# Attention, expert layers and a gated layer on one core: another order of the constant buffers in SBUF

## The chip, the cores and the metric

The kernel runs on one NeuronCore of a Trainium2 chip. The metric is the device time of one execution in microseconds (us). A core has five engines with a queue each: TensorE (PE, matrix products, its weight loads shown as PEld), VectorE (DVE), ScalarE (ACT), GpSimd (POOL) and SyncE (SP, which here only issues DMAs). SBUF is the on-chip memory; a tile takes the same range of bytes in each of 128 partitions, and an address below is an offset in KB inside a partition, as the built program has it.

In a product, PE first loads the *held* operand (up to 128 columns, the `lhsT` of a call), then streams the *moved* operand (`rhs`, 384 or 512 columns) past it. The profile writes `bank<-moved,held`.

## The reference, cut to what matters

```python
def _moe_ref(x, w_gate, w1, w2):            # 1536 tokens, D 512, E 8 experts, F 1024
    P = ...                                 # gates: softmax of x @ w_gate, 8 Sinkhorn rounds
    for e in range(E):
        h = np.maximum(x @ w1[e], 0.0)      # first products, relu
        out += P[:, e:e+1] * (h @ w2[e])    # second products
    return out

def _moe2_ref(x, w_gate, w_val, w_out):     # 512 -> 1536 -> 512
    gate = 1.0 / (1.0 + np.exp(-(x @ w_gate)))
    val = x @ w_val                         # first products, two of them
    return gate * val @ w_out               # second products

def reference(**kwargs):
    x = _attn_ref(...)                      # banded attention, 2 x 8 heads, 768 positions
    return _moe2_ref(_moe_ref(x, ...), ...)
```

## The kernel before

Every large product is done in three passes on pairs of float32r parts (high and low): `product` (lines 360 to 370) emits, for each slice of the contraction, high x high (L368), high x low (L369 moves the low part) and low x high (L370 holds the low part). So each matmul has a weight load of its own, and lines 368 to 370 carry nearly all of PE's work.

The work falls into *visits*, one for each quarter of an expert's hidden width or each sixth of the gated layer's. In a visit **first products** hold slices of a weight tile (`wh[slot][0]`, `wl[slot][0]`) and move tokens (`xh`, `xl`); their results become the hidden pair `hh`, `hl`. **Second products** hold slices of `hh`, `hl` and move the output weights (`wh[slot][1]`, `wl[slot][1]`, 512 columns) into an accumulator `acc`. Second products of one unit run behind the first products of the next.

- Expert 0 runs in plain visits (`run_visit`): first products of 12 matmuls with 384 columns, second products of 6 with 512 columns. The gate's logits (L1166, L1170, held tile `wg2`) lie among them.
- Experts 1 to 7 run in 28 fast visits (`run_fast`, `pair`), each of two halves. A half has 7 products of 6 matmuls with 384 columns, which move `xh`/`xl` or the transformed tokens `th`/`tl` and hold slices (`form`) of `wh00`, `wl00`, `wh10`, `wl10`, and 6 second products of 6 matmuls with 512 columns: 78 matmuls. The order is written out in `pair`.
- The last (gated) layer has 6 blocks of three chunks of 512 tokens. In a chunk, 48 first products with 512 columns are followed by the 24 second products of the chunk before. Even blocks hold `wh*0`/`wl*0`; odd blocks hold four tiles of a pool of their own (`wgh`, `wgl`, `wvh`, `wvl`). The layer's hidden pairs (`hid.extend`, L1302) are also tiles of that pool, `hh0`, `hl0`, `hh1`, `hl1`. The pool (`glu`) opens on the space of the fast visits' pool.

Tiles get addresses in the order in which a pool makes them. The order of instructions is the order of the calls; nothing is rescheduled.

Of the kernel before, what the change touches and what calls it, by code (L numbers as in the profile page):

```python
# [9 lines left out]
F32 = mybir.dt.float32  # L10
F32R = mybir.dt.float32r
# [6 lines left out]
P = 128  # L18
# [7 lines left out]
HID = 3  # L26
# [40 lines left out]
def tile_global_local_attention__then__sinkhorn_moe__then__glu(  # L67
# [27 lines left out]
    E, _, F = w1.shape  # L95
# [3 lines left out]
    KD = DM // P  # L99
# [3 lines left out]
    C = TC * P  # L103
    CM = 4 * P
    CB = S // C
    FQ = 2 * P
# [7 lines left out]
    const = ctx.enter_context(tc.tile_pool(name="const", bufs=1))  # L114
# [5 lines left out]
    ones = const.tile([P, P], F32, name="ones")  # L120
    xh = const.tile([P, KD, N], F32R, name="xh")
    xl = const.tile([P, KD, N], F32R, name="xl")
    accs = [const.tile([P, TB, DM], F32, name="acc0")]
    hh3 = const.tile([P, HID, 2, C], F32R, name="hh3")
    hl3 = const.tile([P, HID, 2, C], F32R, name="hl3")
    hid = [(hh3[:, i], hl3[:, i]) for i in range(HID)]
    wh = [[const.tile([P, 4 * FQ], F32R, name=f"wh{i}{j}") for j in range(2)] for i in range(2)]
    wl = [[const.tile([P, 4 * FQ], F32R, name=f"wl{i}{j}") for j in range(2)] for i in range(2)]
    raw = [const.tile([P, 8 * FQ], F32, name=f"raw{i}") for i in range(2)]

    dram = ctx.enter_context(tc.tile_pool(name="dram", bufs=1, space=bass.MemoryType.DRAM))
    glw = [dram.tile([P, 4 * FQ], F32, name=f"glw{i}") for i in range(3 * NFF)]
    wgr = const.tile([P, KD, E], F32, name="wgr")
    wg2 = const.tile([P, KD, 2 * E], F32R, name="wg2")

    def acc(t):
        return accs[t // TB][:, t % TB, :]
# [490 lines left out]
    with tc.tile_pool(name="attn", bufs=1) as ap:  # L628
# [79 lines left out]
        for h in range(H):  # L708
            j = h % 2
# [270 lines left out]
        with cmp.Else():  # L980
            with tc.tile_pool(name="whole", bufs=1) as gp:
# [15 lines left out]
                for s in range(B * NP):  # L997
                    b, p = divmod(s, NP)
# [16 lines left out]
                    for i in range(NB):  # L1015
# [29 lines left out]
                        for j in range(2):  # L1045
                            h = 2 * (s % NP) + j
# [245 lines left out]
    for step in glu_split[3:6]:  # L1292
# [4 lines left out]
    glu = ctx.enter_context(tc.tile_pool(name="glu", bufs=1))  # L1297
# [1 line left out]
        tuple(glu.tile([P, 4 * FQ], F32R, name=f"w{j}{x}") for x in "hl") for j in "gv"  # L1299
    )  # L1300
    state["glu_hid"] = 0
    hid.extend(  # L1302
        tuple(glu.tile([P, 2, CM], F32R, name=f"h{x}{i}") for x in "hl") for i in range(2)
    )
    state["sg"] = Ring(glu.tile([P, CM], F32, name=f"sg{i}") for i in range(2))
    state["z"] = Ring(glu.tile([P, CM], F32, name=f"z{i}") for i in range(2))
    state["o"] = Ring(glu.tile([P, DM], F32, name=f"o{i}") for i in range(3))
# [57 lines left out]
```

## Time and profile before

| | us |
|---|---|
| median of 3 runs | 1451.95 |
| lowest, highest | 1450.70, 1451.98 |
| the profiled execution's own time | 1453.22 |
| its span, first to last instruction | 1450.7 |

The page of the profile gives each engine's busy time and 40 slices of the span; its chain follows the work that ended last backwards. In the timeline each row is an instruction: start, duration, engine, line, operation, operands and shape. A matmul's duration is modelled and reaches past the start of the next; the distance between two starts is what PE takes for one. Grouped views add instructions of one line and shape up: how many, their busy time, the mean of one.

### The profile page before, as it was taken

To read this page: it belongs to the slowest core of one execution; us is meant where nothing else is said; L and a number is where in the kernel's file an instruction comes from. 1 tells how busy PE (TensorE), PEld (TensorE's weight loads), DVE (VectorE), ACT (ScalarE), POOL (GpSimd) and SP (SyncE) were. 2 spreads that over 40 slices of the span, in tenths; PEclk is the share of its full clock that TensorE was granted. 3 is DMA by queue.
4 is the path that set the end of the run, shared out by engine and by line. 5 is a ranking of instruction groups with operands and counts; after the bars stand their busy time and mean duration, and the time that the engine had idled before them with its cause. 6 is when DMAs were issued, how large, how long until landed. Compare 5 with 4: busy or idle time off the path is not lost.

```text
span 1450.7 us, 19810 instructions
## 1 busy us (share of the span) xinstructions
PE 1432.3 (99%) x7287; PEld 1231.5 (85%) x7287; DVE 863.0 (59%) x1655; ACT 505.3 (35%) x1152; POOL 568.1 (39%) x618
## 2 busy tenths in 40 slices
PE   8999999999999999999999999999999999999998
PEld 4666788999999999999899899899999888888887
DVE  6576477676657666767676666666665533333333
ACT  5777322433333333333333333333333322122111
POOL 3555354554344454354454444445432221112110
PEclk9999999999999999999999999999999999999999
DMA  7661011122121222221212212212210110010002
GB/s 178 160 144 45 17 45 58 45 102 73 52 73 52 73 79 75 73 73 51 73 52 102 73 53 72 73 52 102 73 37 29 44 45 15 30 44 30 0 1 87
DMA packets 99192, 92.60 MB, mean 64 GB/s; under 512 B 55312, under 2 KB 73744, under 8 KB 99088
## 3 DMA queue, kind: packets, MB, share of 16 engines
q1 hardware_dynamic: 98800, 91.26, 20.3%
q8 instruction: 59, 0.97, 0.3%
q14 instruction: 45, 0.37, 0.1%
q10 hardware_dynamic: 288, 0.00, 0.0%
HBM read 78.66 MB, written 12.58 MB: 63 GB/s over the span
## 4 chain that ended last, share of the span: by engine, by line
PE 95%; DVE 2%; ACT 1%; POOL 1%; issue 1%; DMA 0%; DVEq 0%; ACTq 0%; SPq 0%; POOLq 0%
PE bank L368 30%; PE bank L370 30%; PE bank L369 30%; PE bank L867 1%; PE bank L919 1%; PE bank L905 1%; PE bank L841 1%; ACT e L881 1%; DVE e L875 0%; POOL wl L202 0%; PE bank L1313 0%; POOL e L893 0%; DMA lens<-in_n_local_dram 0%; DMA qr<-in_q_dram 0%; DVE kT L845 0%
## 5 line engine op out<-in xcount | busy, mean ns | idle before, releaser
L451 DVE SCALAR_TENSOR_TENSOR acc<-bank,gate,acc 128x512 f32<-128x512 f32 x336 | 251.6, 749 | 234.4 <-PE bank L370 232.1
L370 PE MATMUL bank<-wh,hl 128*128 128x512 f32 x912 | 359.6, 394 | 0.0
L368 PE MATMUL bank<-wh,hh 128*128 128x512 f32 x912 | 359.1, 394 | 0.0
L202 POOL TENSOR_TENSOR wl<-raw,wh 128x512 fp32r<-128x512 f32 (+1 forms) x196 | 209.7, 1086 | 380.3 <-ACT wh L201 380.1
L369 PE MATMUL bank<-wl,hh 128*128 128x512 f32 x912 | 358.0, 392 | 0.0
L368 PE MATMUL bank<-xh,wh 128*128 128x384 f32 (+1 forms) x720 | 252.9, 351 | 1.3 <-ACT aT L906 1.1
L370 PE MATMUL bank<-xh,wl 128*128 128x384 f32 (+1 forms) x720 | 251.2, 349 | 0.0
L369 PE MATMUL bank<-xl,wh 128*128 128x384 f32 (+1 forms) x720 | 250.1, 347 | 0.0
L370 PEld LDWEIGHTS bank<-wh,hl 128*128 128x128 f32 x912 | 171.2, 188 | 38.3
L546 ACT ACTIVATE hh<-kept 128x384 fp32r<-128x384 f32 x168 | 88.2, 525 | 312.1 <-DVE kept L556 312.1
L368 PEld LDWEIGHTS bank<-wh,hh 128*128 128x128 f32 x912 | 171.6, 188 | 27.8 <-issue 1.3
L369 PEld LDWEIGHTS bank<-wl,hh 128*128 128x128 f32 x912 | 171.5, 188 | 26.9
L368 PEld LDWEIGHTS bank<-xh,wh 128*128 128x128 f32 x720 | 135.4, 188 | 15.5 <-issue 1.3
L369 PEld LDWEIGHTS bank<-xl,wh 128*128 128x128 f32 x720 | 135.3, 188 | 13.5 <-DVE xl L1318 0.5
L370 PEld LDWEIGHTS bank<-xh,wl 128*128 128x128 f32 x720 | 135.1, 188 | 5.7
L202 POOL TENSOR_TENSOR wl<-work,wh 128x256 fp32r<-128x256 f32 x112 | 93.8, 839 | 99.6 <-ACT wh L201 96.9
L560 ACT ACTIVATE kept<-bank 128x384 f32<-128x384 f32 x168 | 82.3, 491 | 120.1 <-PE bank L370 120.0
L548 DVE SCALAR_TENSOR_TENSOR hl<-kept,hh 128x384 fp32r<-128x384 f32 x168 | 112.3, 669 | 1.3 <-ACT hh L546 1.3
L370 PE MATMUL bank<-th,wl 128*128 128x384 f32 x336 | 113.1, 337 | 0.0
L368 PE MATMUL bank<-th,wh 128*128 128x384 f32 x336 | 112.5, 335 | 0.0
L369 PE MATMUL bank<-tl,wh 128*128 128x384 f32 x336 | 112.4, 335 | 0.0
L426 DVE TENSOR_TENSOR z<-bank,sg 128x512 f32<-128x512 f32 x36 | 24.9, 691 | 139.3 <-PE bank L370 139.3
(143 smaller groups left out, 1862.2 us busy)
## 6 DMA issues: line engine op xcount, KB each, us to landing
raw<-in_moe_w_dram SPq DMA_DIRECT2D x72, 512.0 KB, 4.3
glw<-work SPq DMA_DIRECT2D x36, 256.0 KB, 2.3
raw<-glw SPq DMA_DIRECT2D x18, 512.0 KB, 3.3
work<-in_moe_w_gate_dram SPq DMA_DIRECT2D x12, 512.0 KB, 4.0
work<-in_moe_w_val_dram SPq DMA_DIRECT2D x12, 512.0 KB, 3.8
work<-in_moe_w_out_dram SPq DMA_DIRECT2D x12, 512.0 KB, 3.8
qr<-in_q_dram SPq DMA_DIRECT2D x32, 96.0 KB, 2.9
kr<-in_k_dram SPq DMA_DIRECT2D x32, 96.0 KB, 2.7
```

Source lines behind the costliest of these rows:

```text
L202: nc.gpsimd.tensor_tensor(out=lo, in0=r, in1=h.bitcast(F32), op=ALU.subtract)
L368: nc.tensor.matmul(lhsT=ah, rhs=bh, start=first, stop=False, **mm)
L369: nc.tensor.matmul(lhsT=ah, rhs=bl, start=False, stop=False, **mm)
L370: nc.tensor.matmul(lhsT=al, rhs=bh, start=False, stop=end, **mm)
L426: nc.vector.tensor_tensor(out=z, in0=ps, in1=sg, op=ALU.mult)
L451: nc.vector.scalar_tensor_tensor(out=a, in0=ps, scalar=gate[:, t, e : e + 1], in1=a, op0=ALU.mult, op1=ALU.add,)
L546: nc.scalar.activation(out=hh[:, f, :C], in_=src, func=AF.Relu)
L548: lambda: nc.vector.scalar_tensor_tensor(out=hl[:, f, :C], in0=src, scalar=0.0, in1=hh[:, f, :C].bitcast(F32), op0=ALU.max, op1=ALU.subtract,)
L560: nc.scalar.activation(out=snap[:, i], in_=ps, func=AF.Copy)
L841: nc.tensor.transpose(ps[:, j * P : (j + 1) * P], raw_[u % QKB][:, j, :], ident)
L867: nc.tensor.matmul(out=ps[j][:, lo:KW], lhsT=qT[rows, own], rhs=kT[rows, keys], start=True, stop=True,)
L881: nc.scalar.activation(out=e[:, j, lo:KW], in_=e[:, j, lo:KW], func=AF.Exp, scale=-1.0, bias=mn[:, j : j + 1], accum_out=rs[:, j : j + 1],)
```

## The change

The constant tiles are made in another order, `hh3`/`hl3` become flat tiles that `hidden_parts` cuts up, and the last layer's two hidden pairs are cut from them too instead of being tiles of the last layer's pool. The addresses in KB of each partition, from the built programs:

| tiles | role | before | after |
|---|---|---|---|
| xh, xl | moved in first products | 17.12 to 65.12 | the same |
| wh01, wl01, wh11, wl11 | moved in second products | 99.12 to 103.12, 115.12 to 119.12, 107.12 to 111.12, 123.12 to 127.12 | 65.12 to 81.12 |
| acc0 | accumulator | 65.12 to 77.12 | 81.12 to 93.12 |
| wgr, wg2 | gate weights, wg2 held | 143.12 to 143.50 | 93.12 to 93.50 |
| hh3, hl3 | held in second products | 77.12 to 95.12 | 93.50 to 111.50 |
| wh00, wl00, wh10, wl10 | held in first products | 95.12 to 99.12, 111.12 to 115.12, 103.12 to 107.12, 119.12 to 123.12 | 111.50 to 127.50 |
| raw0, raw1 | weights as loaded | 127.12 to 143.12 | 127.50 to 143.50 |
| last layer's wgh, wgl, wvh, wvl | held in first products, odd blocks | 156.44 to 172.44 | the same |
| last layer's hh, hl | held in second products | 172.44 to 188.44 | in hh3, hl3 |
| last layer's sg, z, o | scratch | 188.44 to 202.44 | 172.44 to 186.44 |
| th, tl | moved in fast visits | 177.44 to 213.44 | the same |
| acc1 | accumulator | 143.50 to 155.50 | the same |

A multiple of 512 bytes is a multiple of half a KB: a start at .12 is 128 bytes past one, at .44 448 bytes, at .50 none; wg2 starts 256 bytes past one in both.

```diff
+    wh, wl = ([[None, None] for _ in range(2)] for _ in range(2))
+    def weight_tiles(j):
+        for i in range(2):
+            wh[i][j] = const.tile([P, 4 * FQ], F32R, name=f"wh{i}{j}")
+            wl[i][j] = const.tile([P, 4 * FQ], F32R, name=f"wl{i}{j}")
+    weight_tiles(1)
     accs = [const.tile([P, TB, DM], F32, name="acc0")]
-    hh3 = const.tile([P, HID, 2, C], F32R, name="hh3")
-    hl3 = const.tile([P, HID, 2, C], F32R, name="hl3")
-    hid = [(hh3[:, i], hl3[:, i]) for i in range(HID)]
-    wh = [[const.tile([P, 4 * FQ], F32R, name=f"wh{i}{j}") for j in range(2)] for i in range(2)]
-    wl = [[const.tile([P, 4 * FQ], F32R, name=f"wl{i}{j}") for j in range(2)] for i in range(2)]
+    wgr = const.tile([P, KD, E], F32, name="wgr")
+    wg2 = const.tile([P, KD, 2 * E], F32R, name="wg2")
+    hh3 = const.tile([P, HID * 2 * C], F32R, name="hh3")
+    hl3 = const.tile([P, HID * 2 * C], F32R, name="hl3")
+    def hidden_parts(count, m):
+        h, lo = (
+            x[:, 0 : count * 2 * m].rearrange("p (i f m) -> p i f m", i=count, f=2)
+            for x in (hh3, hl3)
+        )
+        return [(h[:, i], lo[:, i]) for i in range(count)]
+    hid = hidden_parts(HID, C)
+    weight_tiles(0)
     raw = [const.tile([P, 8 * FQ], F32, name=f"raw{i}") for i in range(2)]
...
-    wgr = const.tile([P, KD, E], F32, name="wgr")
-    wg2 = const.tile([P, KD, 2 * E], F32R, name="wg2")
...
-    hid.extend(
-        tuple(glu.tile([P, 2, CM], F32R, name=f"h{x}{i}") for x in "hl") for i in range(2)
-    )
+    hid.extend(hidden_parts(2, CM))
```

On every engine the instructions and their order stay as they were. One set of waits moves on PE: that for everything that used the space on which the last layer's pool opens. It stands with the first instruction of PE that reads a tile of that pool. Before, this is the first second product behind the transposes of `acc` (the numbers in the names are the program's own: wh_81 is wh11, hh_12296 the last layer's hh0):

```order
L1313 MATMUL bank_70<-ident,acc_4929 128x128 x3
L368 MATMUL bank_66<-wh_81,hh_12296 128x512 [waits DMAHW4_49,DMAHW3_49,DMAHW5_49,DMAHW2_49,DMAHW6_49,DMAHW1_49,DMAHW7_49,DMAHW0_49,PE_49]
L369 MATMUL bank_66<-wl_85,hh_12296 128x512
L370 MATMUL bank_66<-wh_81,hl_12297 128x512
L368 MATMUL bank_66<-wh_81,hh_12296 128x512
```

In the changed kernel the same place reads a part of hh3 (hh_82, hl_83; wh_77 is wh11), which is no tile of that pool, and has no wait:

```order
L1329 MATMUL bank_70<-ident,acc_4929 128x128 x3
L386 MATMUL bank_66<-wh_77,hh_82 128x512
L387 MATMUL bank_66<-wl_78,hh_82 128x512
L388 MATMUL bank_66<-wh_77,hl_83 128x512
L386 MATMUL bank_66<-wh_77,hh_82 128x512
```

The waits now stand on PE before the first product of the first odd block:

```order
L388 MATMUL bank_67<-wh_77,hl_83 128x512
L386 MATMUL bank_63<-xh,wgh 128x512 [waits DMAHW4_49,DMAHW3_49,DMAHW5_49,DMAHW2_49,DMAHW6_49,DMAHW1_49,DMAHW7_49,DMAHW0_49,PE_49]
L387 MATMUL bank_63<-xl,wgh 128x512
L388 MATMUL bank_63<-xh,wgl 128x512 [waits Pool_49]
L386 MATMUL bank_63<-xh,wgh 128x512
```

Only these waits have moved, from the one place to the other.

## Rows read from the trace of the kernel before

**Rows 1.** Head of the page: busy us, share, instructions; granted clock in 40 slices.

```profile
PE 1432.3 (99%) x7287; PEld 1231.5 (85%) x7287; DVE 863.0 (59%) x1655; ACT 505.3 (35%) x1152; POOL 568.1 (39%) x618
...
PEclk9999999999999999999999999999999999999999
```

**Rows 2.** The page's chain that ended last, shares of the span by engine.

```profile
PE 95%; DVE 2%; ACT 1%; POOL 1%; issue 1%; DMA 0%; DVEq 0%; ACTq 0%; SPq 0%; POOLq 0%
```

**Rows 3.** Busy us by window, last layer: PE, PEld, DVE, ACT, POOL, clock, DMA.

```profile
1240.00:1290.00 50.00, 50.00 (x220) 40.98 (x219) 16.81 (x25) 10.51 (x18) 7.92 (x7) 1.00 0.10 32
```

**Rows 4.** Timeline of PE in the last layer: start us, duration us, instruction.

```profile
1257.55 0.39 PE L368 MATMUL bank<-xh,wh 128*128 128x512 f32 x1
...
1258.94 0.39 PE L368 MATMUL bank<-xh,wh 128*128 128x512 f32 x1
...
1263.02 0.39 PE L368 MATMUL bank<-xh,wh 128*128 128x512 f32 x1
...
1268.46 0.40 PE L368 MATMUL bank<-wh,hh 128*128 128x512 f32 x1
...
1284.97 0.40 PE L368 MATMUL bank<-wh,hh 128*128 128x512 f32 x1
...
1290.57 0.40 PE L368 MATMUL bank<-xh,wgh 128*128 128x512 f32 x1
...
1301.77 0.40 PE L368 MATMUL bank<-wh,hh 128*128 128x512 f32 x1
```

**Rows 5.** Groups of PE in the last layer (1160 to 1451 us): count, busy us, mean ns.

```profile
L368 PE MATMUL bank<-wh,hh 128*128 128x512 f32 x144 | 57.1, 396 | 0.0
...
L368 PE MATMUL bank<-xh,wh 128*128 128x512 f32 x123 | 48.1, 391 | 0.0
...
L368 PE MATMUL bank<-xh,wgh 128*128 128x512 f32 x72 | 28.5, 396 | 0.0
```

**Rows 6.** Timeline of PE from one logit group to the next (x4: four matmuls).

```profile
154.66 1.08 PE L1166 MATMUL bank<-xh,wg 128*16 128x512 f32 x4
...
156.51 0.40 PE L368 MATMUL bank<-wh,hh 128*128 128x512 f32 x1
...
157.89 1.10 PE L1166 MATMUL bank<-xh,wg 128*16 128x512 f32 x4
```

**Rows 7.** Timeline of PE in expert 0, first products of 384 columns.

```profile
208.73 0.33 PE L368 MATMUL bank<-xh,wh 128*128 128x384 f32 x1
...
209.80 0.33 PE L368 MATMUL bank<-xh,wh 128*128 128x384 f32 x1
...
210.97 0.42 PE L368 MATMUL bank<-xh,wh 128*128 128x384 f32 x1
211.23 0.34 PE L369 MATMUL bank<-xl,wh 128*128 128x384 f32 x1
...
212.48 0.33 PE L370 MATMUL bank<-xh,wl 128*128 128x384 f32 x1
```

**Rows 8.** Timeline of PE in a fast visit, the first and last from half to half.

```profile
756.05 0.33 PE L368 MATMUL bank<-xh,wh 128*128 128x384 f32 x1
...
757.12 0.34 PE L368 MATMUL bank<-xh,wh 128*128 128x384 f32 x1
...
758.16 0.33 PE L368 MATMUL bank<-th,wh 128*128 128x384 f32 x1
...
771.70 0.33 PE L368 MATMUL bank<-xh,wh 128*128 128x384 f32 x1
```

**Rows 9.** Timeline of PE where the last layer's first products begin.

```profile
1142.71 0.39 PE L368 MATMUL bank<-xh,wh 128*128 128x512 f32 x1
...
1144.07 0.39 PE L368 MATMUL bank<-xh,wh 128*128 128x512 f32 x1
```

**Rows 10.** Instructions on acc: durations ns min/median/max, first and last start.

```profile
L451 DVE SCALAR_TENSOR_TENSOR acc<-bank,gate,acc x336: 732/751/753, 275.7 to 1142.9; 128x512 f32<-128x512 f32 x168
```

**Rows 11.** DMAs that write glw from the fast visits' pool: first and last start.

```profile
L354 SPq DMA_DIRECT2D glw<-work x36: 326/338/1409, 295.0 to 1070.3; - x36
```

## Prediction

> **What bounds the kernel now.** I read the head of the page first: TensorE (PE) is busy 1432.3 of 1450.7 us, and the clock line is full in every slice [rows 1]; the chain that ended last is 95% PE [rows 2]. The granted clock is 1.00 in the last layer's window too [rows 3], so these matmuls run at the 2.4 GHz level. So the time is the sum of the steps from one matmul start to the next, plus about 18 us in which PE stands still; other engines matter only where PE waits for them. The "busy" of a matmul is modelled and overlaps the next one; I go by differences of starts in the timeline. They are printed to 0.01 us, so I take runs of 6 to 48.
>
> The reader should see in these starts that the same shape does not always take the same step. A 512-column matmul needs 512 / 2.4 GHz = 213.3 ns of columns. In an even block of the last layer, from 1263.02 to 1268.46 us, 24 first products (moved xh/xl, held wh/wl) take 5.44 us: **226.7 ns** each. The second products right behind such a stretch (moved wh/wl, held hh/hl), from 1284.97 to 1290.57 us, are 24 in 5.60 us: **233.3 ns**. The first products of the next, odd block, held wgh/wgl/wvh/wvl, from 1290.57 to 1301.77 us, are 48 in 11.20 us: 233.3 ns again [rows 4]. The grouped view says the same in its modelled durations: 396 ns where hh or wgh is held, 391 where wh is; the groups of L369 and L370 and of the other tiles of odd blocks read alike [rows 5].
>
> What differs is the held buffer. By the address table above, wh*0/wl*0 lie at 95 to 123 KB, wgh to wvl at 156 to 172 KB, the last layer's hh/hl at 172 to 188 KB. The moved ones do not tell: xh/xl (17 to 65 KB) go at 226.7 with one held buffer and 233.3 with the other. A third held buffer above 128 KB is wg2 (143 KB): its eight logit matmuls, four of L1166 and four of L1170, take 1.85 us (154.66 to 156.51), 231 ns each, though they load 16 columns or 8 [rows 6]. So slow held reads begin somewhere between 127 and 143 KB.
>
> **The change part by part.** No instruction is added, removed or moved, so the sum holds only what a new address does to each step.
>
> *Second products of the last layer.* Their hh/hl move from 172 to 188 KB down to 93.5 to 111.5 KB. There are 144 of each of three lines, 432 [rows 5], and each falls from 233.3 to 226.7 ns: 432 x 6.67 = **-2.88 us**. All of it is on the path, since PE has no gaps there [rows 3].
>
> *Entries.* Going from slow seconds into fast firsts costs six matmuls 1.39 us (1257.55 to 1258.94) where settled ones take 1.36 [rows 4]: 0.03 us, about 7 times; this goes: -0.2 us. But wgh to wvl stay where they are, so the seconds of the 9 chunks of odd blocks now come behind slow firsts and pay such an entry themselves: +0.27 us.
>
> *Logits.* wg2 moves from 143 to 93 KB: three groups of eight, 24 x (231.3 - 226.7) = -0.11 us, and the six seconds behind a group (156.51 to 157.89, 1.38 us) lose their 0.02 excess three times [rows 6]: together -0.2 us.
>
> *Expert layers: moved weights down, hidden parts up.* Of seconds there, moved wh*1/wl*1 go from 99 to 127 KB to 65 to 81, held hh/hl from 77 to 95 up to 93.5 to 111.5; held wh*0/wl*0 close up at 111.5 to 127.5. All of these lie below 127.5 KB before and after. One half of a fast visit, 78 matmuls, takes 771.70 - 756.05 = 15.65 us [rows 8]. Six settled 384-column matmuls take 1.04 us (757.12 to 758.16), 173.3 each [rows 8], so 42 x 173.3 + 36 x 226.7 ns = 15.44 us: an excess of 0.21 us in each of 56 halves, **11.8 us** in all. Does it come from the addresses? I think not. At 208.73 us, behind 512-column seconds, six 384-column firsts take 1.07 us instead of 1.04. At 210.97 us a matmul of another kind stalls PE in the middle of equal firsts, and the seven from 211.23 to 212.48 take 1.25 us instead of 1.21 [rows 7]: the same excess, with no change of address. And at 1142.71 us, behind seconds that hold hh3/hl3 in the old place, six firsts of *equal* width take 1.36 us, no excess at all, although moved and held addresses both jump [rows 9]. So the excess follows a stall or a change of width (512 to 384 and back), which stays. I take 0, and keep -11.8 as one end. The other end, in which new places are slow, is priced below.
>
> *Other engines.* acc0 moves by 16 KB. The accumulation took 732 to 753 ns over all 336, half of them into acc1 at 143 KB [rows 10], so between those two places VectorE differs by 21 ns at most, and it is not the bound: 0.
>
> *The moved wait.* One set of waits, on eight DMA queues and PE, leaves the first second product of the last layer and stands before its first wgh product. The last DMA out of the released space was issued at 1070.3 us [rows 11], over 70 us before the last layer's first products at 1142.71 [rows 9]: 0 in either place.
>
> Sum: -2.88 - 0.2 + 0.27 - 0.2 = **-3.0 us**. Against the profiled execution's own 1453.22 us (span 1450.7 and 2.5 us around it) that is 1450.2, a ratio of 0.9979. That execution lies 1.3 us above the median of the runs, 1451.95, so on the median the forecast is **1448.9 us**.
>
> **The rivals.**
>
> *The expert layers gain too.* If the excess comes from seconds holding buffers that lie below what they move (77 to 95 against 99 to 127 KB) while firsts do the opposite, the change makes both alike and up to 11.8 us more goes: 1437. For it: the excess sits at switches between the two kinds. Against it: the switch without excess at 1142.71 us, one instance [rows 9], and the same excess without a switch [rows 7]. The likelier partial result is 1441 to 1446.
>
> *Nothing changes.* The slow step of the last layer might hang on something that goes with those stretches and not on the place, and then the time stays at 1452.0. Against it: even and odd blocks alternate with equal work, and only the held tile differs [rows 4, 5]. The Trainium skill, "TensorE: Matmul & The Clock Gate", section "Wait — 56ns, not 53.3ns?", gives a fixed cost of about 2.5 ns for each matmul on top of its columns and names no part of SBUF in which it differs; by that rule the change would do nothing. The trace does not agree with it: the cost is 13.4 ns with one held buffer and 20.0 with another [rows 4].
>
> *Slower: it is the offset, not the place.* Slow held tiles start 448 bytes past a multiple of 512 (wg2: 256), fast ones 128 past. The change puts hh3, hl3 and wh*0/wl*0 at 0 past, which no row shows. If 0 is as slow as 448, all matmuls of the fast visits go at +6.67: 78 x 6.67 = 0.52 us less the 0.21 they lose now, x 56 = +17.4 us; the even firsts of the last layer add 432 x 6.67 = +2.9, and its seconds gain nothing: **1472**. With no gain left in the last layer, it is slower by a measurable 2.9 us as soon as some 440 matmuls take 6.67 ns more. Against it: wg2 is slow although its slices start at 256, 320, 384 and 448 past.
>
> **How the numbers follow.** Forecast 0.60, expert layers gain too 0.18, nothing 0.10, offset 0.12. A measurement of this kernel tells about 0.2% (2.9 us) from no change, and the forecast of 3.0 lies on that bound: I count a little over half of it (0.33) as faster, 0.27 as the same. Faster 0.33 + 0.18 = 0.51, the same 0.27 + 0.10 = 0.37, slower 0.12. The range takes in forecast and "nothing" and the partial gains of the expert layers: 1441 to 1453; it leaves out the full gain and the offset.
>
> **What would show it.** In the changed profile the last layer's groups that hold hh or hl fall from 396 to 390 or 391 ns while those with wgh to wvl stay at 396; 24 seconds there take 5.44 to 5.47 us; the eight logit matmuls take about 1.81 us; half a fast visit stays at 15.65 us. If that half becomes 15.45, the first rival holds; 16 us, the last. If wg2, which keeps its offset of 256, becomes fast, the place decides and not the offset. Seconds of the last layer still at 5.60 us would make the forecast wrong at its main term.

## The result and the profile after

The changed kernel takes 1461.82 us in the median of 6 runs (1460.49 to 1463.18), the kernel before 1451.43 beside it: a ratio of **1.0068, 95% interval 1.0057 to 1.0078**. It is slower by some 10 us, where 3 us of gain were forecast, and it lies outside the range of 1441 to 1453. Its profiled execution took 1460.91 us, with a span of 1458.5.

The head of the page answers [rows 1]: PE has the same 7287 instructions and is busy 8.3 us longer. The clock line shows a 9 in all 40 slices, before and after. A 9 stands for 90% or more, so it doesn't show whether the clock was full throughout.

```profile
PE 1440.6 (99%) x7287; PEld 1235.8 (85%) x7287; DVE 860.9 (59%) x1655; ACT 505.8 (35%) x1152; POOL 568.9 (39%) x618
```

The timeline of PE at the places of [rows 9] and [rows 4] (start us, duration us, instruction; lines 368 to 370 are now 386 to 388):

```profile
1148.89 0.40 PE L386 MATMUL bank<-xh,wh 128*128 128x512 f32 x1
...
1264.45 0.39 PE L386 MATMUL bank<-xh,wh 128*128 128x512 f32 x1
...
1265.85 0.39 PE L386 MATMUL bank<-xh,wh 128*128 128x512 f32 x1
...
1270.02 0.40 PE L386 MATMUL bank<-xh,wh 128*128 128x512 f32 x1
...
1275.61 0.39 PE L386 MATMUL bank<-wh,hh 128*128 128x512 f32 x1
...
1292.34 0.39 PE L386 MATMUL bank<-wh,hh 128*128 128x512 f32 x1
...
1297.90 0.40 PE L386 MATMUL bank<-xh,wgh 128*128 128x512 f32 x1
...
1309.10 0.39 PE L386 MATMUL bank<-wh,hh 128*128 128x512 f32 x1
```

The reader should take the differences. The 24 seconds from 1292.34 to 1297.90 take 5.56 us where 5.60 stood and 5.44 to 5.47 were forecast: 231.7 ns each. The 24 even-block firsts from 1270.02 to 1275.61 take **5.59 us instead of 5.44**, 232.9 ns each, although neither their moved buffer nor the half of the memory in which their held one lies has changed. The 48 odd-block firsts take 11.20 us as before. The groups of the last layer say the same in their modelled means (count, busy us, mean ns, idle), beside [rows 5]; the last row also shows the moved set of waits costing nothing, idle 0.0:

```profile
L386 PE MATMUL bank<-wh,hh 128*128 128x512 f32 x144 | 56.9, 395 | 0.0
...
L386 PE MATMUL bank<-xh,wh 128*128 128x512 f32 x130 | 51.6, 397 | 0.0
...
L386 PE MATMUL bank<-xh,wgh 128*128 128x512 f32 x72 | 28.4, 395 | 0.0
```

Half a fast visit, beside [rows 8], takes 774.61 - 758.83 = **15.78 us** instead of 15.65, and the other halves of both traces agree with these within 0.03 us. The logit group, beside [rows 6], takes 154.04 - 152.19 = 1.85 us, as before, from its new place below 94 KB:

```profile
152.19 1.08 PE L1184 MATMUL bank<-xh,wg 128*16 128x512 f32 x4
...
154.04 0.39 PE L386 MATMUL bank<-wh,hh 128*128 128x512 f32 x1
...
758.83 0.34 PE L386 MATMUL bank<-xh,wh 128*128 128x384 f32 x1
...
774.61 0.34 PE L386 MATMUL bank<-xh,wh 128*128 128x384 f32 x1
```

Cut at the first product of [rows 7], which lies inside expert 0 (the earlier part of that expert runs among the attention), and at the first product of the last layer, the spans of all kernels of this study are (us, from the starts in the timelines; the kernels k are told below):

| kernel | up to [rows 7]: attention and part of expert 0 | rest of the experts | last layer to the end |
|---|---|---|---|
| before | 208.73 | 933.98 | 307.99 |
| after | 206.51 | 942.38 | 309.61 |
| k1, held tiles 128 bytes on | 206.94 | 934.01 | 305.25 |
| k2, before with held tiles at 0 | 208.47 | 930.09 | 308.04 |
| k3, last layer's part alone | 207.34 | 934.03 | 305.23 |
| k4, all starts alike | 206.40 | 933.59 | 302.21 |
| k5, moved tiles shifted | 212.78 | 934.30 | 303.22 |
| k6, before with the offsets of after | 208.25 | 942.36 | 310.09 |

So the change costs 8.4 us in the experts and 1.6 in the last layer, together about the 10 us by which the medians differ. The first stretch is 2.2 us shorter after the change, which is why the two profiled executions are only 7.7 us apart. Most of that (1.6 us) is the clock. PE stands still for 1.71 us in both kernels, up to 41.23 us before and 40.53 after; then the granted clock (third from the end of each row) averages 0.57 of full speed from 41 to 45 us in the kernel before and is 1.00 in the changed one (before, then after: us, PE busy, clock, DMA share, GB/s):

```profile
41.00:45.00 4.00, 3.77 (x21) 0.57 0.57 128
...
41.00:45.00 4.00, 3.54 (x35) 1.00 0.55 123
```

The profiled executions of k2, k3 and k6, which keep the old order of tiles, also have some 3.4 us at a clock of 0.50 near this place; those of k1, k4 and k5, which have the new one, don't. Whether the order brings that about, or chance, no run tells.

### The profile page after: what moved, and what is told of

Read it like the earlier page. It is cut to its first block, busy times and chain, and to the rows that moved or that the text cites. A ratio compares the mean times of both kernels' runs of the same rounds, so it can differ in the third digit from the quotient of the medians.

```text
span 1458.5 us, 19810 instructions
## 1 busy us (share of the span) xinstructions
PE 1440.6 (99%) x7287; PEld 1235.8 (85%) x7287; DVE 860.9 (59%) x1655; ACT 505.8 (35%) x1152; POOL 568.9 (39%) x618
## 4 chain that ended last, share of the span: by engine, by line
PE 95%; DVE 2%; ACT 1%; POOL 1%; issue 0%; DMA 0%; SPq 0%; DVEq 0%; ACTq 0%; POOLq 0%
PE bank L386 30%; PE bank L387 30%; PE bank L388 30%; PE bank L885 1%; PE bank L937 1%; PE bank L923 1%; PE bank L859 1%; ACT e L899 1%; POOL wl L220 0%; DVE e L893 0%; PE bank L1329 0%; POOL e L911 0%; DMA lens<-in_n_local_dram 0%; ACT aT L924 0%; PE bank L708 0%
```

## The experiments

**The theories.** *Place*: the forecast's own, held tiles above some address are slow; the loss would then come from new places. *Offset*: a held tile that starts at 0 (or 448) bytes past a multiple of 512 is slow, whatever is moved. *Difference*: what counts is the held start minus the moved start, modulo 256 bytes. In the kernel before, the first products that move x (xh, xl) against wh\*0 and the seconds of the experts have difference 0; in the changed one hh3, hl3 and wh\*0 start at 0 and what moves against them (th and tl apart) at 128, so it is 128. By kind of product, the differences are:

| kernel | firsts of xh/xl | firsts of th/tl | seconds, experts | odd-block firsts | seconds, last layer |
|---|---|---|---|---|---|
| before | 0 | 192 | 0 | 64 | 64 |
| after, k6 | 128 | 64 | 128 | 64 | 128 (k6: 64) |
| k1, k3 | 0 | 192 | 0 | 64 | 0 |
| k2 | 128 | 64 | 0 | 64 | 192 |
| k4 | 0 | 0 | 0 | 0 | 0 |
| k5 | 0 | 64 | 0 | 192 | 0 |

**m1: the step by itself.** Fifty-four settings of 48 matmuls each, held and moved slices cut from one buffer at chosen bytes, and no other work of the computation:

```diff
+# moved high, moved low, held high, held low (byte addresses), step of moved and held, columns
...
+    for mh, ml, hh, hl, ms, hs, n in CONFIGS:
+        for g in range(RUN // 12):
...
+                for i, (mv, hd) in enumerate(((a, c), (b, c), (a, d))):
+                    nc.tensor.matmul(
+                        out=ps, lhsT=words(hd, P), rhs=words(mv, n),
```

> A kernel of matmuls alone, in the three-pass order of the real one (held pair, moved pair), 48 in a row for each of 54 settings of addresses; attention, experts and gated layer are left out, so only the steps between starts count, not the total. Main scan: 512 columns, moved at 17 and 41 KB, held at 96 and 112 KB, the held start moved in steps of 64 bytes through 512. Offset theory (only where the held start lies in 512 bytes counts): 226.7 ns a step with held at 128 past, 232 to 234 at most other offsets, the same with moved at 0, 128 or 448 past. Difference theory (held start against moved start): with moved at 0 the fast held offset is 0, with moved at 448 it is 448. Place theory (low moved, held at 94 to 128 KB or not): all offsets alike in the main scan, and held at 156 KB slow at every offset. With held at 156 KB the offset theory expects 226.7 at 128 past.

Pairs of starts 40 matmuls apart, moved slices from 17 KB: held from 96 KB at differences 0, 64, 128 and 192, then held from 156 KB at 0 and 64 (start us, duration us, instruction):

```profile
122.31 0.62 PE L113 MATMUL bank<-big 128*128 128x512 f32 x2
131.39 0.61 PE L113 MATMUL bank<-big 128*128 128x512 f32 x2
...
133.24 0.63 PE L113 MATMUL bank<-big 128*128 128x512 f32 x2
142.57 0.40 PE L113 MATMUL bank<-big 128*128 128x512 f32 x1
...
144.44 0.62 PE L113 MATMUL bank<-big 128*128 128x512 f32 x2
153.74 0.63 PE L113 MATMUL bank<-big 128*128 128x512 f32 x2
...
155.58 0.62 PE L113 MATMUL bank<-big 128*128 128x512 f32 x2
164.74 0.62 PE L113 MATMUL bank<-big 128*128 128x512 f32 x2
...
321.41 0.61 PE L113 MATMUL bank<-big 128*128 128x512 f32 x2
330.47 0.61 PE L113 MATMUL bank<-big 128*128 128x512 f32 x2
...
332.32 0.40 PE L113 MATMUL bank<-big 128*128 128x512 f32 x1
341.66 0.63 PE L113 MATMUL bank<-big 128*128 128x512 f32 x2
```

At 96 KB the 40 steps take 9.08, 9.33, 9.30 and 9.16 us: 227, 233, 232 and 229 ns. At 156 KB they take 9.06 at difference 0 and 9.34 at 64: 226.5 and 233.5. The high place is as fast as the low one, so **the place theory falls**. Settled, with moved starts at 0, 128 and 448 and held starts in steps of 64 over 512 bytes, the steps repeat with 256 bytes: 226.7 at 0, 233.4 at 64, 232.3 at 128 (233.3 in one setting of it), 228.8 at 192. A held start of 0 goes at 226.7 with a moved one of 0 and at 232 to 233 with one of 128: **the offset theory falls** too. With 384 columns 40 steps at difference 128 take 7.04 us, 176.0 ns, and those at 0 take 173.3: there the loss is 2.7 ns, not 6.

Between these steps of 64 the difference alone doesn't settle it. Ten settings with other differences gave 226.7 ns at 144, 240 and 252, 230.7 at 8, and 232.4 to 233.5 at 4, 16, 32, 160, 224 and 248. Every setting at difference 0 went at 226.7 to 226.9.

**k1: the changed kernel with its held tiles 128 bytes further on.**

```diff
+    const.tile([P, 32], F32, name="pad0")
     hh3 = const.tile([P, HID * 2 * C], F32R, name="hh3")
...
     weight_tiles(0)
+    const.tile([P, 96], F32, name="pad1")
```

> The changed kernel with 128 bytes of nothing before hh3 and 384 behind wl10: hh3, hl3, wh*0, wl*0 start 128 bytes past a multiple of 512 again, everything else keeps its offset; places differ by at most half a KB. Offset theory and difference theory: matmuls of the fast visits go back to the steps of the kernel before (half a fast visit 15.65 us) and the last layer's second products fall to 226.7 ns: 1447.5 to 1449.5 us. Place theory: stays at 1461 to 1462 us.

1448.81 us, ratio to before 0.9984 (0.9974 to 0.9993). All of the loss is gone with 128 free bytes (and 384 behind wl10, which keep the offsets of what follows): the experts take 934.01 us as they do before, and the 24 seconds of the last layer 5.44 us:

```profile
1282.13 0.39 PE L388 MATMUL bank<-wh,hh 128*128 128x512 f32 x1
...
1287.57 0.40 PE L388 MATMUL bank<-xh,wgh 128*128 128x512 f32 x1
```

**k2: the kernel before, its held tiles (and wh\*1, wl\*1) moved to 0.** The offset theory wants this slow.

```diff
+    const.tile([P, 96], F32, name="pad0")
     hh3 = const.tile([P, HID, 2, C], F32R, name="hh3")
...
     wl = [[const.tile([P, 4 * FQ], F32R, name=f"wl{i}{j}") for j in range(2)] for i in range(2)]
+    const.tile([P, 32], F32, name="pad1")
```

> The kernel before with 384 bytes of nothing before hh3 and 128 behind wl11: all of hh3, hl3, wh, wl start on a multiple of 512, in the order and places of before. Offset theory: as slow as the changed kernel, 1460 to 1464 us, and the last layer's first products of even blocks go from 226.7 to some 233 ns. Difference theory: first products slow (held 0, moved 128), but second products of the expert layers (held 0, moved 0) fast, so 1455 to 1459 us. Place theory: unchanged, 1450.5 to 1452.5 us.

1448.35 us, ratio 0.9979 (0.9969 to 0.9988): faster, not slower. The last layer parts the theories most plainly:

```profile
1259.16 0.39 PE L370 MATMUL bank<-xh,wh 128*128 128x512 f32 x1
...
1264.72 0.39 PE L370 MATMUL bank<-wh,hh 128*128 128x512 f32 x1
...
1281.35 0.39 PE L370 MATMUL bank<-wh,hh 128*128 128x512 f32 x1
...
1286.85 0.39 PE L370 MATMUL bank<-xh,wgh 128*128 128x512 f32 x1
```

Even firsts (difference 128) take 5.56 us where before they took 5.44, in the same place to half a KB. The seconds, whose held hh/hl have moved by no more than half a KB and still start 448 past, take 5.50 instead of 5.60, 229.2 ns, because what *moves* against them did: difference 192, which m1 puts at 228.8. The difference theory's own 1455 to 1459 us missed too, by 6.7 us: it left out that the excess at the changes of width can go (the sum below; half a visit takes 15.57 us here).

**k3: the last layer's part alone**, in the kernel before (its hidden pairs cut from hh3/hl3, no tile made in another order).

```diff
...
+    hh3 = const.tile([P, HID * 2 * C], F32R, name="hh3")
+    hl3 = const.tile([P, HID * 2 * C], F32R, name="hl3")
...
-    hid.extend(
-        tuple(glu.tile([P, 2, CM], F32R, name=f"h{x}{i}") for x in "hl") for i in range(2)
-    )
+    hid.extend(hidden_parts(2, CM))
```

> The kernel before with one part of the change alone: the last layer's hidden pairs are cut from hh3 and hl3 in their old place (77 KB, 128 bytes past a multiple of 512) instead of lying at 172 KB (448 past). Offset theory, difference theory and the forecast's own theory of a border between 127 and 143 KB all expect its 432 second products to fall from 233.3 to 226.7 ns: 1448 to 1449.5 us. If neither offset nor place of held tiles matters there, 1451.4 us.

1449.07 us, ratio 0.9980 (0.9970 to 0.9989), last layer 307.99 - 305.23 = 2.76 us shorter. It can't be told from k1, which has all the new places: at equal differences the new order of tiles is worth nothing.

**k6: the kernel before in its own places, with the offsets of the changed one.** Free bytes ahead of hh3 and between the weight tiles; no tile moves by more than 2 KB.

```diff
+    const.tile([P, 96], F32, name="pad")
     hh3 = const.tile([P, HID, 2, C], F32R, name="hh3")
...
+    for x, w in (("h", wh), ("l", wl)):
+        for i in range(2):
+            for j in range(2):
+                w[i][j] = const.tile([P, 4 * FQ], F32R, name=f"w{x}{i}{j}")
+                if (x, i, j) != ("l", 1, 1):
+                    const.tile([P, 96 if j else 32], F32, name=f"pad{x}{i}{j}")
```

> The kernel before, in its own order and places, with free bytes between the tiles so that each starts at the offset modulo 256 that it has in the kernel after: hh3, hl3, wh*0, wl*0 at 0, wh*1, wl*1, xh, xl at 128; th, tl and the last layer's tiles stay at 448. Each tile moves by at most 2 KB. Difference theory: the whole loss of the change comes back without the change: second products and first products at a difference of 128, those that move th/tl at 64; 1461 to 1463. The last layer's second products stay at 64 (20.1 instead of 19.0), worth +0.4. Place theory: the loss comes from the new places, so the time stays at 1451 to 1452.

1462.82 us, ratio 1.0069 (1.0052 to 1.0086): the whole loss without the change. The experts take 942.36 us (after: 942.38), half a visit 15.79 us, the even firsts 5.57:

```profile
760.55 0.34 PE L374 MATMUL bank<-xh,wh 128*128 128x384 f32 x1
...
776.34 0.34 PE L374 MATMUL bank<-xh,wh 128*128 128x384 f32 x1
...
1271.85 0.40 PE L374 MATMUL bank<-xh,wh 128*128 128x512 f32 x1
...
1277.42 0.40 PE L374 MATMUL bank<-wh,hh 128*128 128x512 f32 x1
```

**k5: the changed kernel, held tiles left at 0, the moved ones shifted to 0.**

```diff
+    const.tile([P, 96], F32, name="pad0")
     xh = const.tile([P, KD, N], F32R, name="xh")
...
     weight_tiles(1)
+    const.tile([P, 32], F32, name="pad1")
```

> The kernel after, with 384 bytes left free before xh and 128 behind the first weight tiles: the moved xh, xl, wh*1 and wl*1 now start at 0 modulo 512, and the held hh3, hl3 and wh*0 stay at 0, where the kernel after has them. Difference theory: difference 0 again for first and second products, so 2707 second products go from 18.5 to about 16.3 ns over their columns (-6.0 us), 423 first products of the last layer's even blocks from 19.2 to 14 (-2.2), 432 of the odd blocks from 19.9 to 15.4 (their difference becomes 192: -1.9), 1714 short ones from 17.0 to 16.4 (-1.0); the 1008 that move th/tl stay at 17.2: 1461.8 - 11 = about 1450.5. Offset theory (a held start of 0 is slow, whatever is moved): nothing changes, 1461 to 1462. Place theory: nothing changes either, 1461 to 1462.

1452.62 us, ratio 0.9994 (0.9975 to 1.0012), some 9 to 11 us below the changed kernel and 2 above the 1450.5 expected. Its ten runs spread from 1445.63 us, at a granted clock of 1.000, to 1456.75, at 0.995. In the profiled execution the first stretch is 6 us longer than that of the changed kernel, and the trace shows with what: at 171 us one small VectorE instruction (L1227, 128x12) took 8.43 us, where the same one took 1.57 to 1.63 in the other seven kernels. PE stood still for 4.41 us behind it, and the clock right after that was 0.50, the 1.2 GHz level; why the instruction was slow isn't shown.

```profile
180.40 0.74 PE L1235 MATMUL bank<-gate,ones 128*128 128x96 f32 x2 [4.41 <-DVE gate L1229]
...
180.40:185.90 5.50, 5.50 (x14) 0.50 0.55 191
```

So the median alone says little about this layout. Past [rows 7], experts and last layer take 1237.52 us against 1251.99: 14.5 us less, where 11 were expected. Held exactly where the changed kernel holds them, even firsts take 5.44 us and seconds 5.44, and the odd firsts (difference now 192) 10.99 instead of 11.20:

```profile
1265.90 0.39 PE L388 MATMUL bank<-xh,wh 128*128 128x512 f32 x1
...
1271.34 0.39 PE L388 MATMUL bank<-wh,hh 128*128 128x512 f32 x1
...
1287.66 0.39 PE L388 MATMUL bank<-wh,hh 128*128 128x512 f32 x1
...
1293.10 0.39 PE L388 MATMUL bank<-xh,wgh 128*128 128x512 f32 x1
...
1304.09 0.39 PE L388 MATMUL bank<-wh,hh 128*128 128x512 f32 x1
```

**k4: every difference 0** (wg2 apart): k1, and 192 bytes more in the pool `late`, behind which th, tl and the last layer's tiles lie, so that these start at 128 as well.

```diff
+    late.tile([P, 48], F32, name="pad2")
```

> The kernel after with 128 bytes left free before hh3 and 192 bytes before the last layer's wgh to wvl and before th/tl, so that every tile that a matmul holds and every tile that it moves starts at the same place modulo 256 bytes (wg2 alone sweeps all of them). Difference theory (a matmul's step is set by held start minus moved start, modulo 256 bytes: 13.3 ns over its columns at 0, 20.1 at 64, 19.0 at 128, 15.5 at 192): on top of what the 128 bytes alone gave (1448.8), the 432 first products of the odd blocks fall from 20.0 to 13.3 ns over their columns, 432 x 6.67 = 2.9 us, so 1445.5 to 1446.5. Place theory (slow above some address): the odd blocks still hold wgh to wvl above 150 KB, so they stay at 20 and the time stays at 1448.8. Offset theory (only the held start counts): also about 1446, so this run does not part it from the first.

**1445.07 us, ratio 0.9951 (0.9934 to 0.9967)**: the lowest median of the study, some 7 us below the kernel before and just under the 1445.5 to 1446.5 expected. The odd firsts, held above 156 KB, take 10.88 us for 48, 226.7 ns each:

```profile
1285.59 0.39 PE L388 MATMUL bank<-xh,wgh 128*128 128x512 f32 x1
...
1296.47 0.39 PE L388 MATMUL bank<-wh,hh 128*128 128x512 f32 x1
```

**m2: which pair counts, and changes of width.** Again matmuls alone, with starts that alternate, widths that alternate, and a finer scan.

> Everything but matmuls is left out: 144 groups of 12 matmuls back to back, which load a 128-column held tile each time, on a buffer filled once. First, moved starts alternate between 0 and 64 (or 128) bytes, held starts too, in step or crossed, so that either a matmul's own two starts agree or its moved start and the next matmul's held start do. If loading the next held tile while the current one moves is what collides, then the crossed order (own starts unequal, next ones equal) goes at 13.3 ns over its columns and the order in step goes at the mean of 64 and 192, about 17.8; if a matmul's own pair counts, the other way round. Second, six matmuls of 384 columns and six of 512 in turn, at a difference of 0: if the excess of 0.21 us in a half fast visit comes from the change of width, each turn loses some 30 ns in its first matmuls; if not, all stay at 13.3. Third, a scan of the difference in steps of 16 bytes at 512 columns: 13.3 near 0 within 16 bytes below it, 20 from 16 to 112 above, falling to 15.5 at 192. Fourth, 0, 64, 128 and 192 at 384 and at 256 columns.

Starts 24 matmuls apart: widths in sixes at difference 0 and at 64, then 384 columns alone at difference 0 and at 64:

```profile
96.83 0.51 PE L198 MATMUL bank<-big 128*128 128x384 f32 x2
101.69 0.51 PE L198 MATMUL bank<-big 128*128 128x384 f32 x2
...
126.12 0.52 PE L198 MATMUL bank<-big 128*128 128x384 f32 x2
131.04 0.52 PE L198 MATMUL bank<-big 128*128 128x384 f32 x2
...
145.41 0.51 PE L198 MATMUL bank<-big 128*128 128x384 f32 x2
149.57 0.51 PE L198 MATMUL bank<-big 128*128 128x384 f32 x2
...
153.77 0.52 PE L198 MATMUL bank<-big 128*128 128x384 f32 x2
158.01 0.52 PE L198 MATMUL bank<-big 128*128 128x384 f32 x2
```

Of 24 matmuls, half of each width, 4.86 us are 0.06 more than 12 x (173.3 + 226.7) ns: 0.03 us for each six-and-six, with no address changing its offset. So a change of width does cost at difference 0, as the prediction had it. At difference 64 it doesn't: 24 matmuls take 4.92 us, which is 12 x (176.7 + 233.3) ns, and at 128 they take 4.91, again the sum of the steps of the two widths. With 384 columns, difference 64 takes 4.24 us for 24, 176.7 ns, against 173.3 at 0. The first part was not decided: with a matmul's own two starts alike and its neighbours' not, the step was 231.6 (starts 0 and 64) and 228.3 ns (0 and 128); crossed it was 233.3 and 230.0. Neither order came to 226.7, so neither pair alone sets the step. The scan came out ragged as well: 226.7 within 16 bytes on either side of 0, 232 to 234 from 32 to 160, 230.0 at 176, 228.9 at 192, 233.3 at 208 and 224. In m1 differences of 16, 128 and 144 went at 233.4, mostly 232.3 and 226.7, in m2 at 226.7, 233.3 and 233.3: off 0 a stretch can settle in more than one pattern. And with 256 columns the order turns: 120.0 ns at 0, 117.8 at 64.

**The sum, put together.** With the settled steps of m1 and m2, half a fast visit (24 firsts of x, 18 of t, 36 seconds) can be worked out and set beside the timelines:

| kernel | settled steps, ns: x, t, seconds | us worked out | us in the timeline |
|---|---|---|---|
| before, k1 | 173.3, 173.3, 226.7 | 15.44 | 15.65 |
| after | 176.0, 176.7, 232.4 | 15.77 | 15.78 |
| k6 | the same | 15.77 | 15.79 |
| k2 | 176.0, 176.7, 226.7 | 15.56 | 15.57 |
| k5 | 173.3, 176.7, 226.7 | 15.50 | 15.65 |
| k4 | 173.3, 173.3, 226.7 | 15.44 | 15.64 |

Where the firsts of x run at difference 0, the half has 0.15 to 0.21 us more than its settled steps; five turns of 0.03 are 0.15. Where they run at 128 (after, k6, k2), this excess is no longer there. m2 shows the same without the computation: width changes cost 0.03 us a turn at difference 0 and nothing at 64 and 128. That is how k2's half is the shortest although k4's differences are all 0. Why a difference takes the cost of the turns away, and why it does so in k2, whose seconds stay at 0, no run tells.

## Why the prediction was wrong, point by point

**What bounds the kernel: right.** PE, one step after another; the loss is all in the steps. "Full in every slice" read more than the line shows: the clock averaged 0.57 from 41 to 45 us. The last layer's 1.00 [rows 3] stands.

**"So slow held reads begin somewhere between 127 and 143 KB": the step that failed.** The two sorts of step were read rightly (226.7 and 233.3 ns, [rows 4]), but of the things in which the tiles differ the place was picked. The offset went with it in nearly every row (wg2 apart): held tiles below 128 KB start at 128 like what moves against them, those above at 448. "The moved ones do not tell" is the mistake in small: xh/xl go fast with one held buffer and slow with another, which says that the moved one *alone* doesn't decide, and it was taken to say that it plays no part. m1, k2, k5 and k6 show that it does: what sets the step is the difference of the two starts, 226.7 ns at 0 and 233.4 at 64, held at 96 KB or at 156 (m1).

**Seconds of the last layer, -2.88 us: the size was right, the condition not met.** At difference 0 they do gain it: k3's last layer is 2.76 us shorter, k1's 2.74. In the change they go from difference 64 to 128, 233.3 to 231.7 ns by the 24 shown: 432 x 1.6 = -0.7 us. The mean over the whole layer is 233.3 to 232.4, so -0.4.

**Even firsts: counted at nothing, cost +2.7 by the 24 shown** (432 x (232.9 - 226.7) ns), on a difference of 128 in a tile that only "closed up". The mean over the layer, 227.5 to 232.5, gives +2.2; with the seconds' -0.4 that is 1.8, near the 1.6 by which the layer is longer.

**Entries, -0.2 and +0.27:** six matmuls into an even block take 1.40 us (1264.45 to 1265.85) like any six of that block now; there is no entry left to see. Small either way.

**Logits, -0.2: failed.** The group takes 1.85 us from 93 KB as it did from 143. Its slices lie 64 bytes apart and so run through all four differences; the mean of 226.7, 233.4, 232.3 and 228.8 is 230.3 ns, near its 231 (an estimate, since m1 holds 128 columns and wg2's slices are 16 or 8). The prediction had named this as the test ("If wg2, which keeps its offset of 256, becomes fast, the place decides"), and it spoke against the place.

**Expert layers, 0: failed, +8.4 us.** Matched step by step from [rows 7] on (steps over 0.26 us left out), 2133 seconds rose by 1.7 ns, 1008 firsts of t by 4.1 and 1487 of x by 0.5: together 8.4 us. The seconds rose by less than m1's 5.7 ns because the excess at the changes of width went. The firsts of t show it in the grouped view too, before and then after (count, busy us, mean ns, idle):

```profile
L368 PE MATMUL bank<-th,wh 128*128 128x384 f32 x336 | 112.5, 335 | 0.0
```

```profile
L386 PE MATMUL bank<-th,wh 128*128 128x384 f32 x336 | 114.3, 340 | 0.0
```

The argument on the excess of 0.21 us held in part: width changes do cost 0.03 a turn at fixed offsets (m2). That it "stays" did not hold: at differences 64 and 128 it is gone (m2), which softens the loss.

**The other engines and the moved wait, 0: right.** acc took 733 to 754 ns beside [rows 10] (`min/median/max` in the row), and the first odd block's product shows no idle time.

```profile
L469 DVE SCALAR_TENSOR_TENSOR acc<-bank,gate,acc x336: 733/750/754, 274.2 to 1149.1; 128x512 f32<-128x512 f32 x168
```

**The rivals.** "It is the offset, not the place" came nearest: it named the 0 past which held tiles now start, and the right sign. Two things in it were wrong. Its counter-argument, wg2 slow at four offsets, was the best evidence *for* a dependence on bytes: slices at 256, 320, 384 and 448 are a sweep. And its price, 1472, put 6.67 ns on every matmul: the half visit was to lose 0.52 us, and by m1 and m2 it loses 24 x 2.7 + 18 x 3.4 + 36 x 5.7 ns = 0.33, less the 0.21 as the rival had it: about 0.12 us, measured 0.13. "The expert layers gain too" would have needed the excess to go without the loss. "Nothing changes" went by the Trainium skill, "TensorE: Matmul & The Clock Gate", section "Wait — 56ns, not 53.3ns?", with its fixed 2.5 ns or so on each matmul; here even the best stretch of 512 columns has 13.3 ns over its columns (m1), and the rest depends on the bytes at which the two operands start, so the measurement decides against a fixed cost for these streams.

## What to carry to other kernels

Before a layout is changed for its places, write down each tile's start modulo 256 bytes, and for each stream of matmuls with a weight load of their own the difference between held and moved start; a tile made one place earlier can shift all that follow, and here 128 free bytes (k1) were worth some 12 us. Equal starts are the safe choice at 512 columns, the one difference that went fast in every setting (k4: three pads, some 7 us below the kernel before), but at narrow or mixed widths measure, since 256 columns and k2's half visits say otherwise. And where two features go together in every row of a trace, a blind forecast should price both and give the second more than 0.12; matmuls alone at chosen starts (m1) told them apart in one run.

## What the runs showed of the hardware

- The step of back-to-back matmuls that each load 128 held columns depends on the held start minus the moved start modulo 256 bytes: at 512 columns 226.7, 233.4, 232.3 and 228.8 ns at 0, 64, 128 and 192. Between these it isn't a rule: 144 went at 226.7 in m1 and at 233.3 in m2. Whether anything in the chip collides, and what, was not found.
- It doesn't depend on the place: held tiles at 96 and at 156 KB, moved ones at 17 and at 160 KB gave the same steps.
- The price depends on the width: at 64 bytes it is 6.7 ns at 512 columns, 3.4 at 384, and at 256 columns difference 0 is the slower one by 2.2 ns.
- A change of width costs about 0.03 us for each six-and-six of 384 and 512 columns at difference 0, and nothing at 64 and at 128 (m2).
- A stop of PE can be followed by some us at half the granted clock, and need not be: after the same 1.7 us stop it was 0.57 on average in the kernel before and 1.00 in the changed one.
